# Eight column orders for the moving operands of the up- and down-projection matmuls

## The chip, the cores and the metric

The kernel runs on one core of a Trainium2 chip. The metric is the device time of one launch in microseconds. Three timed runs of the kernel before gave 1766.06, 1766.77 and 1769.52 us (median 1766.77 us). The profile is of one further execution.

## What is computed

Batch 8, sequence 3136, model width 256, feed-forward width 1024; x is float32, and the feed-forward weights are double precision. A spectral layer comes first, then a gated feed-forward layer with a convolution of three taps along the sequence:

```python
X = np.fft.rfft(x, axis=1)
Yr = Xr @ w_r - Xi @ w_i + b_r
Yi = Xr @ w_i + Xi @ w_r + b_i
Y  = soft_threshold(Yr, 0.01) + 1j * soft_threshold(Yi, 0.01)
x  = np.fft.irfft(Y, n=3136, axis=1)

h = np.maximum(x @ w_in, 0)                     # up-projection, 256 -> 1024
conv_out = sum(conv_w[k] * hp[:, k:k+S] for k in range(3))   # hp: h with a zero at each end
gate = 1 / (1 + np.exp(-conv_out))
out  = (h * gate) @ w_out                       # down-projection, 1024 -> 256
```

## The kernel before

The program has two parts. The first (to about 550 us) does the transforms and the channel mix as matmuls: L245 and L260 (stage 1), L280 (stage 2), L304 (mix) and L331 (stage 3), with results sent through device memory. The second part, where the change lies, runs the last transform (L423, plain float32) and the feed-forward layer.

In the second part the sequence lies along the free axis. `y` holds the transformed input of one batch item twice, `yh` (rounded to the type float32r, a 4-byte number that TensorE takes in one pass) and `yl` (what the rounding left), each with 128 channels on the partitions, two tiles of channels, and 3168 columns. The weights `win` and `wout` are likewise held as a rounded part and a rest.

The work is cut into 28 chunks of two pieces of 448 positions, and each chunk into 8 blocks `f` of 128 feed-forward channels: 224 steps. A step does the following.

- `up(f, ...)`: for each of the two pieces, six matmuls at L442 into one PSUM bank of the tile `ps_h` (two tiles of channels, times the three products high x high, high x rest, rest x high). The weights of the block are the stationary operand; 450 columns of `yh` or `yl` (448 and one neighbour at each end) are the moving operand, read in order and written to 450 PSUM columns in order. So twelve matmuls of 450 columns for a step.
- ScalarE and VectorE make the activation from it: ReLU out of PSUM into `h` (L444), the three taps (L447 or L449, L451), the sigmoid (L452), the product (L453), and its split into `gh` and `gl` (L456, L457).
- `down(ci, f, ...)`, four steps behind `up` (`LAG = 4`): for each of seven groups of 128 positions, three matmuls at L470. The activation is stationary; 256 columns of `wout`, block f, are moving, and the 256 results are added to half a bank of the accumulators `acc`, in which all eight blocks f are summed. So twenty-one matmuls of 256 columns for a step. After the last block, ScalarE copies the accumulators out (L479) and a DMA stores them.

The order on each engine is made by a scheduler that works from a modelled timeline. TensorE's stream alternates between the twelve matmuls of an `up` and the twenty-one of a `down`, with groups of sixteen L423 matmuls between them for the next batch item. The two PSUM banks of `ps_h` exist twice, so that the next `up` fills one pair while L444 reads the other.

Of the kernel before, what the change touches and what calls it, by code (L numbers as in the profile page):

```python
# [31 lines left out]
CH = 448  # L32
# [64 lines left out]
def spectral_ffn_kernel(ctx: ExitStack, tc: tile.TileContext, x, w_r, w_i, b_r, b_i,  # L97
                        w_in, conv_w, w_out, fwd1, fwd2, inv1, inv2, out):
    nc = tc.nc
# [316 lines left out]
    def stage4(b, jg, y):  # L416
# [10 lines left out]
        def view(q):  # L427
            return q[:, :, 1:S + 1].rearrange("p t (m j) -> p t m j", j=H)[:, :, :, jg * JG:(jg + 1) * JG]
        nc.scalar.copy(view(y[0]), src)
        nc.vector.tensor_tensor(view(y[1]), src, view(y[0].bitcast(F32)), op=ALU.subtract)  # L430

    def up(f, halves):
        ps = psh.tile([P, 2, 512], F32, name="ps_h", tag="ps_h")
        w = slice(f * P, (f + 1) * P)
        for a, (y, c0) in enumerate(halves):
            mm = []
            for t in range(NT):
                mm.append((win[0][:, t, w], y[0][:, t, c0:c0 + CH + 2]))
                mm.append((win[0][:, t, w], y[1][:, t, c0:c0 + CH + 2]))
                mm.append((win[1][:, t, w], y[0][:, t, c0:c0 + CH + 2]))  # L440
            for n, (lt, rh) in enumerate(mm):
                nc.tensor.matmul(ps[:, a, 0:CH + 2], lt, rh, start=(n == 0), stop=(n == len(mm) - 1))  # L442
        h = hp.tile([P, 2, CH + 2], F32, name="h")
        nc.scalar.activation(h, ps[:, :, 0:CH + 2], AF.Relu)  # L444
        c = wk.tile([P, 2, CH], F32, name="c", bufs=3)
        if f in TAP_DVE:
            nc.vector.tensor_scalar_mul(c, h[:, :, 0:CH], cw[:, 0, f:f + 1])  # L447
        else:
            nc.scalar.mul(c, h[:, :, 0:CH], cw[:, 0, f:f + 1])  # L449
        for k in (1, 2):  # L450
            nc.vector.scalar_tensor_tensor(c, h[:, :, k:k + CH], cw[:, k, f:f + 1], c, op0=ALU.mult, op1=ALU.add)  # L451
        nc.scalar.activation(c, c, AF.Sigmoid)  # L452
        nc.vector.tensor_tensor(c, h[:, :, 1:CH + 1], c, op=ALU.mult)  # L453
        gh = wk.tile([P, 2, CH], F32R, name="gh", bufs=5)
        gl = wk.tile([P, 2, CH], F32R, name="gl", bufs=5)
        nc.scalar.copy(gh, c)  # L456
        nc.vector.tensor_tensor(gl, c, gh.bitcast(F32), op=ALU.subtract)  # L457
        return [q.rearrange("p a n -> p (a n)") for q in (gh, gl)]
# [4 lines left out]
    def down(ci, f, gs, acc):  # L463
        gh, gl = gs
        if f == 0:
            acc = [pso.tile([P, 2, D], F32, name=f"acc{k}") for k in range((NM + 1) // 2)]
        for m in range(NM):
            sl = slice(m * P, (m + 1) * P)
            for n, (lt, rh) in enumerate(((gh, wout[0]), (gh, wout[1]), (gl, wout[0]))):
                nc.tensor.matmul(acc[m // 2][:, m % 2, :], lt[:, sl], rh[:, f, :], start=(f == 0 and n == 0 and m % 2 == 0),  # L470
                                 stop=(f == NF - 1 and n == 2), skip_group_check=True)
        if f == NF - 1:
            o = io.tile([P, NM, D], F32, name="o", bufs=1)
            for k, q in enumerate(acc):
                w = min(2, NM - 2 * k)
                if ci == NCH - 1 and k % 2:
                    nc.vector.tensor_copy(o[:, 2 * k:2 * k + w, :], q[:, 0:w, :])
                else:
                    nc.scalar.copy(o[:, 2 * k:2 * k + w, :], q[:, 0:w, :])  # L479
                if ci == NCH - 1:  # L480
                    nc.sync.dma_start(outv[:, ci * NM + 2 * k:ci * NM + 2 * k + w, :], o[:, 2 * k:2 * k + w, :])
            if ci < NCH - 1:
                nc.sync.dma_start(outv[:, ci * NM:(ci + 1) * NM, :], o)
        return acc
# [16 lines left out]
    for st in range(n_st + LAG):  # L501
        if st < n_st:
            ci, f = divmod(st, NF)
            hv = [divmod(2 * ci + a, NH) for a in range(2)]
            if f == 0:
                nb = hv[1][0] + 1
                if nb < B and nb not in ys and hv[0][0] == hv[1][0]:
                    ys[nb] = new_y(nb)
                    todo = [(nb, jg) for jg in range(NPC)]
            gs[st] = up(f, [(ys[b], a * CH) for b, a in hv])  # L510
            if todo and f in (1, 4, 7):
                b, jg = todo.pop(0)
                stage4(b, jg, ys[b])
        if st >= LAG:
            ci, f = divmod(st - LAG, NF)
            accs = down(ci, f, gs.pop(st - LAG), accs)
# [24 lines left out]
```

## Time and profile before

| | before |
|---|---|
| median of three timed runs | 1766.77 us |
| the profiled execution as timed | 1769.05 us |
| its span in the trace | 1767.3 us |
| mean granted TensorE clock | 0.995 |
| first L442 matmul | 574.0 us |
| last L470 matmul starts | 1762.7 us |

Each group of the profile's table stands for one line, one engine and one pair of operands: `out<-in`, the partitions and columns, the count, then the busy time in us and the mean duration of one in ns, then the idle time in front of it. Successive matmuls overlap, so a mean duration is longer than the time from one start to the next; the chain of work that ended last has its pieces cut so that they follow one another.

### The profile page before, as it was taken

The numbers are of one execution on the slowest core, as the hardware profiler recorded it, in microseconds if no ns is written. First come the engines' busy times: TensorE is split into PE (matmuls) and PEld (weight loads), VectorE is DVE, ScalarE is ACT, GpSimd is POOL, SyncE is SP. The second block draws the span as 40 slices with busy tenths as digits, with TensorE's granted clock in tenths as the row PEclk, the third lists the DMA queues.
The fourth block names the chain that finished last, engine by engine and source line by source line (L and its number), as shares of the span: only waits on it lengthen the run. The fifth ranks groups of instructions, "written<-read, shape, count | busy, mean of one in ns | idle before, by whom it ended". The sixth has DMA issues, their size and how long they took to land.

```text
span 1767.3 us, 29387 instructions
## 1 busy us (share of the span) xinstructions
PE 1731.0 (98%) x12096; PEld 1621.6 (92%) x12096; DVE 1524.3 (86%) x1820; ACT 1229.1 (70%) x1590; POOL 134.7 (8%) x60
## 2 busy tenths in 40 slices
PE   6899999999998999999999999999999999999999
PEld 2788888888998999999999999999999999999998
DVE  2899999998896988988888888888888888888887
ACT  2667777776665777777777777777777777777766
POOL 0122222222232000000000000000000000000000
PEclk8999999999999999999999999999999999999999
DMA  9777677677534110111111011111101111100001
GB/s 263 216 230 236 196 232 216 192 230 228 164 111 136 43 43 22 32 53 53 32 53 53 22 55 51 49 46 52 43 22 43 53 43 43 42 22 22 22 22 42
DMA packets 107382, 164.63 MB, mean 93 GB/s; under 512 B 8816, under 2 KB 86000, under 8 KB 107248
## 3 DMA queue, kind: packets, MB, share of 16 engines
q1 hardware_dynamic: 107248, 162.74, 30.9%
q8 instruction: 96, 1.57, 0.4%
q14 instruction: 38, 0.31, 0.1%
HBM read 85.65 MB, written 77.07 MB: 92 GB/s over the span
## 4 chain that ended last, share of the span: by engine, by line
PE 93%; DMA 3%; DVE 1%; ACT 1%; issue 0%; SPq 0%; ACTq 0%
PE acc L470 31%; PE ps_h L442 31%; PE ps_mx L304 12%; PE ps_s L423 5%; PE ps_s L280 5%; PE ps_s L331 4%; PE ps_s L245 4%; DMA i_raw<-in_inv_dram 2%; DMA z<-sc 1%; DMA sc<-ha 0%; DMA a<-sc 0%; DMA sc<-a 0%; ACT a L246 0%; DVE cw L212 0%; DVE yl L430 0%
## 5 line engine op out<-in xcount | busy, mean ns | idle before, releaser
L470 PE MATMUL acc<-wout,gh 128*128 128x256 f32 x3136 | 567.0, 280 | 0.0
L451 DVE SCALAR_TENSOR_TENSOR c<-h,cw,c 128x896 f32<-128x896 f32 x448 | 513.1, 1147 | 47.3 <-ACT c L449 46.3
L442 PE MATMUL ps_h<-yh,win 128*128 128x450 f32 x1792 | 551.0, 368 | 0.1
L470 PEld LDWEIGHTS acc<-wout,gh 128*128 128x128 f32 x3136 | 493.7, 188 | 6.5
L470 PE MATMUL acc<-wout,gl 128*128 128x256 f32 x1568 | 437.6, 281 | 0.0
L444 ACT ACTIVATE h<-ps_h 128x900 f32<-128x900 f32 x224 | 207.7, 927 | 254.8 <-PE ps_h L442 254.8
L442 PEld LDWEIGHTS ps_h<-yh,win 128*128 128x128 f32 x1792 | 338.7, 189 | 26.4 <-DVE yl L430 0.8
L442 PE MATMUL ps_h<-yl,win 128*128 128x450 f32 x896 | 329.2, 367 | 0.0
L470 PEld LDWEIGHTS acc<-wout,gl 128*128 128x128 f32 x1568 | 293.7, 188 | 0.1
L457 DVE TENSOR_TENSOR gl<-c,gh 128x896 fp32r<-128x896 f32 x224 | 243.1, 1089 | 53.6 <-ACT gh L456 50.1
L453 DVE TENSOR_TENSOR c<-h,c 128x896 f32<-128x896 f32 x224 | 243.6, 1088 | 46.9 <-ACT c L452 46.7
L456 ACT CAST gh<-c 128x896 fp32r<-128x896 f32 x224 | 209.8, 942 | 49.4 <-DVE c L453 49.4
L452 ACT ACTIVATE c<-c 128x896 f32<-128x896 f32 x224 | 213.3, 952 | 23.9 <-DVE c L451 21.0
L304 PE MATMUL ps_mx<-wmix_lo,fh 128*128 128x256 f32 x672 | 202.2, 301 | 0.0
L304 PE MATMUL ps_mx<-wmix_hi,fh 128*128 128x256 f32 x672 | 196.9, 294 | 0.5 <-DVE v L313 0.3
L304 PE MATMUL ps_mx<-wmix_hi,fl 128*128 128x256 f32 x672 | 188.7, 282 | 1.3 <-DVE fl L288 1.2
L442 PEld LDWEIGHTS ps_h<-yl,win 128*128 128x128 f32 x896 | 168.9, 189 | 11.0
L449 ACT ACTIVATE c<-h,cw 128x896 f32<-128x896 f32 x168 | 175.5, 1044 | 2.6 <-DVE gl L457 0.2
L321 POOL TENSOR_TENSOR sl<-v,sh 128x1024 fp32r<-128x1024 f32 x56 | 134.5, 2402 | 423.1 <-PE ps_s L331 300.0
L313 DVE TENSOR_TENSOR v<-ps_mx,p 64x512 f32<-64x512 f32 x224 | 154.0, 688 | 3.3
L304 PEld LDWEIGHTS ps_mx<-wmix_lo,fh 128*128 128x128 f32 x672 | 126.4, 188 | 12.3 <-issue 12.3
L304 PEld LDWEIGHTS ps_mx<-wmix_hi,fl 128*128 128x128 f32 x672 | 126.0, 188 | 11.8 <-issue 9.9
(84 smaller groups left out, 2023.0 us busy)
## 6 DMA issues: line engine op xcount, KB each, us to landing
a<-sc SPq DMA_DIRECT2D x56, 448.0 KB, 5.0
sc<-z SPq DMA_DIRECT2D x56, 448.0 KB, 3.3
z<-sc SPq DMA_DIRECT2D x56, 448.0 KB, 3.8
xr<-in_x_dram SPq DMA_DIRECT2D x55, 448.0 KB, 4.7
out_dram<-o SPq DMA_DIRECT2D x27, 896.0 KB, 4.0
sc<-a SPq DMA_DIRECT2D x49, 448.0 KB, 4.9
sc<-ha SPq DMA_DIRECT2D x7, 448.0 KB, 7.5
win_bits<-in_moe_w_in_dram SPq DMA_DIRECT2D x4, 512.0 KB, 7.6
```

Source lines behind the costliest of these rows:

```text
L304: nc.tensor.matmul(ps[c][:, k, :], lt, rh, start=(n == 0), stop=(n == len(mm) - 1))
L313: nc.vector.tensor_tensor(v[dst, :, k, :], ps[c][src], p1[src, c], op=ALU.add)
L321: SL_ENG.tensor_tensor(sl, v, sh.bitcast(F32), op=ALU.subtract)
L442: nc.tensor.matmul(ps[:, a, 0:CH + 2], lt, rh, start=(n == 0), stop=(n == len(mm) - 1))
L444: nc.scalar.activation(h, ps[:, :, 0:CH + 2], AF.Relu)
L449: nc.scalar.mul(c, h[:, :, 0:CH], cw[:, 0, f:f + 1])
L451: nc.vector.scalar_tensor_tensor(c, h[:, :, k:k + CH], cw[:, k, f:f + 1], c, op0=ALU.mult, op1=ALU.add)
L452: nc.scalar.activation(c, c, AF.Sigmoid)
L453: nc.vector.tensor_tensor(c, h[:, :, 1:CH + 1], c, op=ALU.mult)
L456: nc.scalar.copy(gh, c)
L457: nc.vector.tensor_tensor(gl, c, gh.bitcast(F32), op=ALU.subtract)
L470: nc.tensor.matmul(acc[m // 2][:, m % 2, :], lt[:, sl], rh[:, f, :], start=(f == 0 and n == 0 and m % 2 == 0), stop=(f == NF - 1 and n == ...
```

## The change

Two tables, `UP_WALK` and `DOWN_WALK`, give for each block f a pair (b, n), and `walk` views a run of columns as (a, b, n) and then goes over b first, a second, n last. The same view is put on the moving operand and on the PSUM output of a matmul, so each result goes to the column where it went before, and the columns are only visited in another order: n neighbours, a jump over b x n columns, and so on to the end, then again from the next group of n. Block 0 keeps the plain order.

| f | up: run of n columns, jump | down: run of n columns, jump |
|---|---|---|
| 0 | plain | plain |
| 1 | 2, 18 columns (72 bytes) | 2, 4 columns (16 bytes) |
| 2 | 2, 30 (120) | 2, 8 (32) |
| 3 | 2, 50 (200) | 2, 16 (64) |
| 4 | 2, 150 (600) | 2, 32 (128) |
| 5 | 10, 50 (200) | 2, 128 (512) |
| 6 | 30, 150 (600) | 16, 32 (128) |
| 7 | 50, 150 (600) | 64, 128 (512) |

```diff
+    UP_WALK = (None, (9, 2), (15, 2), (25, 2), (75, 2), (5, 10), (5, 30), (3, 50))
+    DOWN_WALK = (None, (2, 2), (4, 2), (8, 2), (16, 2), (64, 2), (2, 16), (2, 64))
+
+    def walk(ap, run):
+
+        return ap if run is None else ap.rearrange("p (a b n) -> p b a n", b=run[0], n=run[1])
+
     def up(f, halves):
...
             for n, (lt, rh) in enumerate(mm):
-                nc.tensor.matmul(ps[:, a, 0:CH + 2], lt, rh, start=(n == 0), stop=(n == len(mm) - 1))
+                nc.tensor.matmul(walk(ps[:, a, 0:CH + 2], UP_WALK[f]), lt, walk(rh, UP_WALK[f]), start=(n == 0), stop=(n == len(mm) - 1))
...
             for n, (lt, rh) in enumerate(((gh, wout[0]), (gh, wout[1]), (gl, wout[0]))):
-                nc.tensor.matmul(acc[m // 2][:, m % 2, :], lt[:, sl], rh[:, f, :], start=(f == 0 and n == 0 and m % 2 == 0),
+                nc.tensor.matmul(walk(acc[m // 2][:, m % 2, :], DOWN_WALK[f]), lt[:, sl], walk(rh[:, f, :], DOWN_WALK[f]), start=(f == 0 and n == 0 and m % 2 == 0),
                                  stop=(f == NF - 1 and n == 2), skip_group_check=True)
```

The new lines move L442 to L449 and L470 to L477. The next rows show TensorE's program at one place of the second part, where the `down` of block 7 is interrupted by the `up` of block 3; `win_78` and `win_79` are the rounded part and the rest of `win`, `wout_80` and `wout_81` those of `wout`. Before:

```order
L470 MATMUL acc_7735<-wout_80,gh 128x256
L470 MATMUL acc_7735<-wout_81,gh 128x256
L470 MATMUL acc_7735<-wout_80,gl 128x256
L442 MATMUL ps_h<-yh,win_78 128x450
L442 MATMUL ps_h<-yl,win_78 128x450
L442 MATMUL ps_h<-yh,win_79 128x450
```

The same place with the change:

```order
L477 MATMUL acc_7735<-wout_80,gh 128x2x2x64
L477 MATMUL acc_7735<-wout_81,gh 128x2x2x64
L477 MATMUL acc_7735<-wout_80,gl 128x2x2x64
L449 MATMUL ps_h<-yh,win_78 128x25x9x2
L449 MATMUL ps_h<-yl,win_78 128x25x9x2
L449 MATMUL ps_h<-yh,win_79 128x25x9x2
```

No row has moved; the shape of the operand has become 25 x 9 x 2 and 2 x 2 x 64 (b, a, n) in place of 450 and 256. Some steps on, again on TensorE, the `down` of block 2 ends and the `up` of block 7 begins:

```order
L477 MATMUL acc_8148<-wout_80,gh 128x4x32x2
L477 MATMUL acc_8148<-wout_81,gh 128x4x32x2
L477 MATMUL acc_8148<-wout_80,gl 128x4x32x2
L449 MATMUL ps_h<-yh,win_78 128x3x3x50
L449 MATMUL ps_h<-yl,win_78 128x3x3x50
L449 MATMUL ps_h<-yh,win_79 128x3x3x50
```

These stood there before as rows of 256 and 450 columns of L470 and L442. On the other engines the rows are the same, in the same order, but for the line numbers.

## The prediction

> **What bounds the kernel now.** I read the page's busy shares and its chain of waits first, since they say which engine sets the end and on which lines.
>
> ```profile
> span 1767.3 us, 29387 instructions
> PE 1731.0 (98%) x12096; PEld 1621.6 (92%) x12096; DVE 1524.3 (86%) x1820; ACT 1229.1 (70%) x1590; POOL 134.7 (8%) x60
> ...
> PE 93%; DMA 3%; DVE 1%; ACT 1%; issue 0%; SPq 0%; ACTq 0%
> PE acc L470 31%; PE ps_h L442 31%; PE ps_mx L304 12%; PE ps_s L423 5%; PE ps_s L280 5%; PE ps_s L331 4%; PE ps_s L245 4%; DMA i_raw<-in_inv_dram 2%; DMA z<-sc 1%; DMA sc<-ha 0%; DMA a<-sc 0%; DMA sc<-a 0%; ACT a L246 0%; DVE cw L212 0%; DVE yl L430 0%
> ```
>
> TensorE is the chain: 93% of the span, and two lines, the up-projection L442 and the down-projection L470, hold 31% each. These are the two lines that the change rewrites, so whatever it does to a matmul's pace is multiplied by thousands. Next I asked for the busy time of the whole feed-forward part, from the first L442 matmul at 574.0 us to the end, and for who waits there.
>
> ```profile
> core 0: us, PE busy (x) PEld busy (x) DVE busy (x) ACT busy (x) POOL busy (x), PEclk, DMA share, GB/s
> 574.00:1767.30 1193.30, 1188.88 (x8147) 1143.87 (x8146) 1034.19 (x1026) 855.76 (x998) 0.00 (x0) 1.00 0.13 40
> ```
>
> ```profile
> ACT h L444 <- PE ps_h L442: 254.8, 175, 3.0
> ...
> PEld ps_h L442 <- DVE yl L430: 0.8, 2, 0.5
> ```
>
> TensorE is busy 1188.88 of 1193.30 us at full granted clock: 4.4 us idle, so there is no slack in which a slower matmul could hide. ScalarE spends 254.8 us waiting for L442's result, while the only wait on TensorE's side is 0.8 us of its weight loads; VectorE works 1034 of 1193 us. A slower TensorE therefore makes the others wait longer and the kernel longer, one for one; a faster one would have about 159 us before VectorE's own work (1034.19 us) becomes the bound.
>
> **What one matmul costs.** The page's mean durations must not be used for this: they are those of single, overlapping instructions. The chain of waits in a short stretch gives the pace.
>
> ```profile
> 1002.82 2.47 PE ps_h L442 x12
> 1005.29 2.48 PE acc L470 x21
> 1007.77 2.47 PE ps_h L442 x12
> 1010.24 2.48 PE acc L470 x21
> ```
>
> Columns are start, length and line in us: twelve up matmuls take 2.47 us (0.206 us each, against 0.368 in the table), twenty-one down matmuls 2.48 us (0.118 each, against 0.280). A step is one feed-forward block of one chunk; there are 28 chunks of 8 blocks, 224 steps, and 224 x 2.47 = 553 us and 224 x 2.48 = 556 us agree with 31% of 1767.3. The counts and sizes are in the table of groups:
>
> ```profile
> L470 PE MATMUL acc<-wout,gh 128*128 128x256 f32 x3136 | 567.0, 280 | 0.0
> ...
> L442 PE MATMUL ps_h<-yh,win 128*128 128x450 f32 x1792 | 551.0, 368 | 0.1
> ...
> L470 PE MATMUL acc<-wout,gl 128*128 128x256 f32 x1568 | 437.6, 281 | 0.0
> ...
> L442 PE MATMUL ps_h<-yl,win 128*128 128x450 f32 x896 | 329.2, 367 | 0.0
> ```
>
> Per column that is 2470/(12 x 450) = 0.457 ns up and 2480/(21 x 256) = 0.461 ns down: proportional to the columns, with next to nothing fixed per instruction. Now the same figure for matmuls that the change does not touch:
>
> ```profile
> 402.22 3.04 PE ps_mx L304 x26
> 405.26 1.42 PE ps_s L331 x12
> 406.68 0.86 PE ps_s L245 x2
> ```
>
> L304 and L331 also move 256 columns of the same rounded 4-byte type: 3040/(26 x 256) = 0.457 ns and 1420/(12 x 256) = 0.462 ns, with other operands, other PSUM tiles and other neighbours. L245 moves 512 columns of plain float32: 860/(2 x 512) = 0.840 ns, the slow pace of this trace for streams of such a length. So two paces exist, and what decides between them is the number type, not where the data lie or what the other engines do.
>
> **The change, part by part.**
>
> *Instructions, order, waits.* Each matmul stays one matmul of the same column count, with the same weights, and the programs of all engines hold the same rows in the same order; only line numbers and the shape of 7 in 8 of the L442 and L470 operands differ. No DMA, wait, weight load, ScalarE or VectorE instruction is added, removed or moved. Cost 0.
>
> *Block 0.* Its order is None for both projections: 28 x (2.47 + 2.48) = 139 us of matmuls as before. Cost 0.
>
> *Blocks with long runs.* Up has runs of 10, 30 and 50 columns (f = 5, 6, 7), down runs of 16 and 64 (f = 6, 7). A break comes at most every 10 columns; if each cost a whole column time, this would be (45 + 15 + 9) runs x 336 matmuls x 0.457 ns + (16 + 4) x 588 x 0.461 ns = 10.6 + 5.4 = 16 us. I take 0, for the reason below.
>
> *Blocks of pairs.* Up f = 1 to 4 and down f = 1 to 5 go in runs of two columns, 8 bytes, with jumps of 72 to 600 bytes (up) and 16 to 512 bytes (down). They hold 4 x 28 x 2.47 = 276.6 us and 5 x 28 x 2.48 = 347.2 us: 623.8 us of matmuls ride on the one thing that this trace does not show, the pace of a TensorE stream that is not contiguous. Every moving operand and every matmul output of the kernel before is contiguous. So I bound it from both sides.
>
> Lower end: the pace is set by the type, as the four lines above show, so a different order gains at most the spread between them: 0.461 against 0.457 ns, 1% of the 7 x 28 x 2.48 = 486 us of reordered down matmuls, 5 us. Upper end: the pairs go at the slow pace of the trace, L245's 0.840 ns. An up step then takes 12 x 450 x 0.840 = 4.54 us (+2.07), a down step 21 x 256 x 0.840 = 4.52 us (+2.04): 4 x 28 x 2.07 + 5 x 28 x 2.04 = 232 + 286 = +518 us.
>
> Between them stand the only scattered accesses of the trace, made by other engines: L429 and L430 read PSUM with 448 bytes between neighbours, where L444 reads it, and L457 reads SBUF, in a straight line.
>
> ```profile
> L457 DVE TENSOR_TENSOR gl<-c,gh 128x896 fp32r<-128x896 f32 x224 | 243.1, 1089 | 53.6 <-ACT gh L456 50.1
> ...
> L444 ACT ACTIVATE h<-ps_h 128x900 f32<-128x900 f32 x224 | 207.7, 927 | 254.8 <-PE ps_h L442 254.8
> ...
> L429 ACT CAST yh<-ps_s 128x896 fp32r<-128x896 f32 x56 | 64.6, 1156 | 10.1 <-PE ps_s L423 10.0
> L430 DVE TENSOR_TENSOR yl<-ps_s,yh 128x896 fp32r<-128x896 f32 x56 | 64.3, 1150 | 14.5 <-ACT yh L429 14.3
> ```
>
> VectorE loses 1150/1089 = 6%, ScalarE 1156/896 against 927/900 per element = 25%, although every single element there is a jump (and the other side of both instructions, the tile y, goes in runs of four). Carried over to 623.8 us that is +35 to +156 us. TensorE would jump at every second column, every 0.91 ns, while these two take 1.28 and 1.29 ns per element: so they do not prove its pace, but they are far nearer to no loss than to L245's 84%. I take **no cost** as the likeliest: the scattered rows lose little with a jump at every element, and pairs halve the jumps. Both ends stay in the range.
>
> [...]
>
> **The sum.** 0 + 0 + 0 + 0 against the profiled execution: 1769.05 us as timed, 1767.3 us of it span. The median of the three timed runs is 1766.77 us, with 1766.06 to 1769.52 around it, so the profile is no special run and the forecast is the median, **1767 us**.
>
> **The rivals.**
>
> 1. *Pairs starve the array* (slower). The place is the nine pair blocks; the price is the slow pace, +518 us, 2285 us. It decides as soon as one 8-byte visit takes longer than two column times, 0.91 ns. For it: TensorE's fast pace leaves no reserve that the trace shows. Against it: the scattered rows lose 6 to 25%, not 84%. Only in down-projection, whose jumps are all powers of two where up's are odd multiples of 8 bytes, it would be +286 us, 2053 us.
> 2. *A partial loss*, of the size that the scattered rows show, or one lost beat at some breaks: +35 to +156 us, 1802 to 1923 us; I name 1862 us. The extreme of one lost column time at every break is (4 x 225 + 69) x 336 x 0.457 ns + (5 x 128 + 20) x 588 x 0.461 ns = 149 + 179 = +328 us, 2095 us.
> 3. *Every broken order is slow*, long runs too: 7 x 28 x (2.07 + 2.04) = +806 us, 2573 us. Against it: with runs of 50 or 64 a jump comes once in 23 or 29 ns. [...]
> 4. *Faster*: at most the 5 us above, 1762 us. Nothing shortens a stream whose column count stays.
> 5. *The change does not do what it says*: not possible for the shapes, which are in the built program; but if the reordered pattern were walked as a contiguous one by the hardware, the time would be that of the forecast.
>
> **How the numbers follow.** No cost: 0.53. Partial loss, anything above 0.2% up to 2095 us: 0.19. Pairs slow in down alone: 0.07; in both: 0.12. Every order slow: 0.06. Faster: 0.03. About 0.2% (3.5 us) is what a measurement of this kernel can tell from no change; a loss of 0.6 ns per reordered matmul (3.5 us over 6468) is enough to leave that band. Hence faster 0.03, same 0.53, slower 0.44. The range runs from 1761 us (the gain bound) to 2100 us (one column time per break, and pairs slow in down alone); above it lie 0.18.
>
> **What would show it.** The new profile splits itself by shape: the chain's pieces give twelve up matmuls and twenty-one down matmuls for each block, and block 0 is the control. Right: all pieces stay at 2.45 to 2.50 us, ScalarE's wait for L444 stays near 255 us and TensorE's busy time near 1731 us. Rival 1 shows pieces of about 4.5 us for pair blocks alone and a wait of ScalarE that grows by hundreds of us; in down alone, only the twenty-ones grow. Rival 2 shows pieces of 2.6 to 3.1 us, growing with the number of runs if each break has a price. Rival 3 shows the runs of 50 and 64 slow as well. The forecast is wrong if any block's piece leaves 2.5 us by more than 0.02 us: 28 x 7 x 2 such pieces would be 8 us.

## The result

The changed kernel takes 2335.36 us (median of four runs, 2333.89 to 2336.66) against 1768.14 us: a ratio of 1.3193, 95% interval 1.3173 to 1.3212. The forecast was no change. The profiled execution has a span of 2334.3 us, 567 us more than before.

The page of the changed kernel, busy shares and chain:

```profile
span 2334.3 us, 29387 instructions
PE 2295.9 (98%) x12096; PEld 1891.9 (81%) x12096; DVE 1530.8 (66%) x1820; ACT 1232.2 (53%) x1590; POOL 134.7 (6%) x60
...
PE 95%; DMA 3%; DVE 1%; ACT 1%; issue 0%; SPq 0%; ACTq 0%; DVEq 0%
```

The same 12096 matmul records keep TensorE busy for 2295.9 us in place of 1731.0; VectorE and ScalarE do the same work in nearly the same time (1530.8 us after 1524.3, and 1232.2 after 1229.1) and only wait longer. The busy time from the first up matmul (576.6 us) to the end, and ScalarE's wait for the up-projection (L442 and L444 are now L449 and L451):

```profile
576.60:2334.30 1757.70, 1753.43 (x8146) 1413.09 (x8145) 1040.64 (x1026) 858.96 (x998) 0.00 (x0) 1.00 0.09 27
```

```profile
ACT h L451 <- PE ps_h L449: 817.5, 224, 8.1
...
PEld ps_h L449 <- issue: 180.3, 844, 0.2
```

The stage has grown from 1193.3 to 1757.7 us at full granted clock, so 564 of the 567 us lie in it, and ScalarE's wait has grown by 563 us. The 180.3 us of TensorE's weight loads stand under issue, which names no engine that they waited for. The chain of one chunk shows which blocks grew; columns are start, length and line, and the sixteen L423 records of the next batch item and the pieces of up block 5 and down blocks 0 and 1 are left out:

```profile
1383.71 2.47 PE ps_h L449 x12
1386.19 4.80 PE acc L477 x21
1390.99 5.09 PE ps_h L449 x12
...
1397.86 3.62 PE acc L477 x21
1401.48 5.12 PE ps_h L449 x12
1406.60 2.52 PE acc L477 x21
1409.13 5.08 PE ps_h L449 x12
1414.21 2.45 PE acc L477 x21
1416.66 3.54 PE ps_h L449 x12
...
1430.39 2.65 PE ps_h L449 x12
1433.05 4.90 PE acc L477 x21
1437.95 2.55 PE ps_h L449 x12
1440.50 4.61 PE acc L477 x21
```

The up pieces are blocks 0 to 4, then 6 and 7; the down pieces run four blocks behind: 4 to 7, then 2 and 3. Plain block 0 stays at 2.47 us for its twelve matmuls; pairs take 5.1 us, runs of 30 and 50 columns 2.65 and 2.55. Two blocks of pairs are much cheaper than the rest: up block 4 (3.54 us) and down block 5 (3.62 us).

The matmul starts in the trace, grouped by block, give the mean time from one start to the next in ns (each block has 336 up and 588 down matmuls). The two rows of visits are a count that is explained below:

| block f | 0 | 1 | 2 | 3 | 4 | 5 | 6 | 7 |
|---|---|---|---|---|---|---|---|---|
| up before | 206 | 206 | 207 | 206 | 206 | 206 | 205 | 205 |
| up after | 208 | 423 | 425 | 422 | 295 | 243 | 224 | 214 |
| up: visits to 16-byte lines x 1.83 ns | 207 | 411 | 411 | 411 | 411 | 247 | 219 | 214 |
| down before | 119 | 117 | 118 | 119 | 117 | 120 | 118 | 118 |
| down after | 120 | 231 | 232 | 220 | 230 | 173 | 121 | 118 |
| down: visits x 1.83 ns | 117 | 234 | 234 | 234 | 234 | 234 | 117 | 117 |

Added up against means of 205.8 and 118.2 ns: up pairs 741 ns x 336 = 249 us, up long runs 63 x 336 = 21 us, down pairs 494 x 588 = 291 us, down long runs 3 x 588 = 2 us; together 562 of the 567 us.

### The profile page after: what moved, and what is told of

Its sections match the earlier page's. It is cut to its first block, busy times and chain, and to the rows that moved or that the text cites. A ratio compares the mean times of both kernels' runs of the same rounds, so it can differ in the third digit from the quotient of the medians.

```text
span 2334.3 us, 29387 instructions
## 1 busy us (share of the span) xinstructions
PE 2295.9 (98%) x12096; PEld 1891.9 (81%) x12096; DVE 1530.8 (66%) x1820; ACT 1232.2 (53%) x1590; POOL 134.7 (6%) x60
## 4 chain that ended last, share of the span: by engine, by line
PE 95%; DMA 3%; DVE 1%; ACT 1%; issue 0%; SPq 0%; ACTq 0%; DVEq 0%
PE acc L477 36%; PE ps_h L449 35%; PE ps_mx L304 9%; PE ps_s L423 4%; PE ps_s L280 4%; PE ps_s L245 3%; PE ps_s L331 3%; DMA i_raw<-in_inv_dram 1%; DMA wm_raw<-in_w_i_dram 0%; DVE v L313 0%; DMA z<-sc 0%; DMA xr<-in_x_dram 0%; DMA sc<-ha 0%; DMA a<-sc 0%; PE ps_s1h L260 0%
## 5 line engine op out<-in xcount | busy, mean ns | idle before, releaser
L477 PE MATMUL acc<-wout,gh 128*128 128x256 f32 x3136 | 815.5, 353 | 0.0
L449 PE MATMUL ps_h<-yh,win 128*128 128x450 f32 x1792 | 743.1, 479 | 0.0
L451 ACT ACTIVATE h<-ps_h 128x900 f32<-128x900 f32 x224 | 206.7, 923 | 817.5 <-PE ps_h L449 817.5
L477 PEld LDWEIGHTS acc<-wout,gh 128*128 128x128 f32 x3136 | 581.3, 198 | 67.3 <-issue 26.3
L477 PE MATMUL acc<-wout,gl 128*128 128x256 f32 x1568 | 551.3, 353 | 0.0
L449 PEld LDWEIGHTS ps_h<-yh,win 128*128 128x128 f32 x1792 | 356.1, 199 | 170.9 <-issue 126.1
L449 PE MATMUL ps_h<-yl,win 128*128 128x450 f32 x896 | 428.5, 478 | 0.0
L477 PEld LDWEIGHTS acc<-wout,gl 128*128 128x128 f32 x1568 | 310.2, 198 | 17.3 <-issue 0.2
L449 PEld LDWEIGHTS ps_h<-yl,win 128*128 128x128 f32 x896 | 178.1, 199 | 74.7 <-issue 54.2
L304 PE MATMUL ps_mx<-wmix_lo,fh 128*128 128x256 f32 x672 | 202.2, 301 | 0.0
L304 PE MATMUL ps_mx<-wmix_hi,fh 128*128 128x256 f32 x672 | 196.9, 294 | 0.5 <-DVE v L313 0.3
L304 PE MATMUL ps_mx<-wmix_hi,fl 128*128 128x256 f32 x672 | 188.6, 282 | 1.3 <-DVE fl L288 1.2
L304 PEld LDWEIGHTS ps_mx<-wmix_lo,fh 128*128 128x128 f32 x672 | 126.4, 188 | 12.3 <-issue 12.3
L304 PEld LDWEIGHTS ps_mx<-wmix_hi,fl 128*128 128x128 f32 x672 | 126.1, 188 | 11.8 <-issue 9.9
```

Source lines behind the costliest of these rows:

```text
L304: nc.tensor.matmul(ps[c][:, k, :], lt, rh, start=(n == 0), stop=(n == len(mm) - 1))
L449: nc.tensor.matmul(walk(ps[:, a, 0:CH + 2], UP_WALK[f]), lt, walk(rh, UP_WALK[f]), start=(n == 0), stop=(n == len(mm) - 1))
L477: nc.tensor.matmul(walk(acc[m // 2][:, m % 2, :], DOWN_WALK[f]), lt[:, sl], walk(rh[:, f, :], DOWN_WALK[f]), start=(f == 0 and n == 0 and ...
```

## The experiments

The **line theory** came out of that table. It supposes that TensorE fetches the moving operand in lines of 16 bytes, four float32r columns, and that a visit to a line takes as long as four columns of the plain stream, 4 x 0.457 = 1.83 ns, however few of its columns are used. The size and the price are an estimate of mine, fitted to the table: pairs take twice the plain time (423 against 206 ns up), runs of 10, 30 and 50 columns 18, 9 and 4% more. Straight on, 450 columns are 113 visits and 256 are 64. In pairs they are 225 and 128. A run of 10 starting 0 or 8 bytes into a line covers 3 lines, 135 visits in all; runs of 30 and 50 cover 8 and 13 lines, 120 and 117 visits; aligned runs of 16 and 64 need no extra visit. But for up block 4 and down block 5 the counts lie within about 6% of the measured pace. Rivals: the loss is in the PSUM writes; or each jump has a price (some 0.9 ns), wherever it lands.

**Reads or writes.** In the first kernel only the moving operand is walked, in the second only the output; the other side is `plain`, the same three-dimensional view without the exchange of a and b. The line theory prices reads alone: by it the first kernel keeps the whole loss and the second has none of it.

```diff
-  nc.tensor.matmul(walk(ps[:, a, 0:CH + 2], UP_WALK[f]), lt, walk(rh, UP_WALK[f]), ...
+  nc.tensor.matmul(plain(ps[:, a, 0:CH + 2], UP_WALK[f]), lt, walk(rh, UP_WALK[f]), ...     # reads only
+  nc.tensor.matmul(walk(ps[:, a, 0:CH + 2], UP_WALK[f]), lt, plain(rh, UP_WALK[f]), ...     # writes only
```

> Only the moving operand is walked in the eight orders; the PSUM output is written straight on, so the sums land in permuted columns (computation changed there). Line theory (TensorE fetches the moving operand in 16-byte lines at 1.83 ns a visit, as long as four columns of 0.457 ns, however few columns a visit uses): the whole loss stays, about 2335 us, pair blocks 0.42 us per up and 0.23 us per down matmul. PSUM theory (the loss is in the 8-byte writes): about 1767 us, all up matmuls 0.206 us. Shared: something between.

> Only the PSUM output is walked; the moving operand is read straight on, so the sums land in permuted columns (computation changed there). [...] PSUM theory: about 2335 us. If any broken write pattern slows a matmul, down blocks 1 to 5 stand at 0.2 us and more.

Reads only: 2334.16 us, ratio 1.3182 (1.3146 to 1.3218). Writes only: 1769.84 us, ratio 0.9998 (0.9985 to 1.0011). The chain of the reads-only kernel, and then of the writes-only kernel:

```profile
1130.69 4.79 PE acc L481 x21
1135.49 5.06 PE ps_h L453 x12
```

```profile
1107.79 2.47 PE ps_h L453 x12
1110.26 2.47 PE acc L481 x21
1112.73 2.47 PE ps_h L453 x12
```

With the reads walked, each block has the pace of the changed kernel within 0.3 ns; with the writes walked, each has the pace of before. The whole loss is on the read side, and none of these orders costs anything in PSUM (ratio 0.9998).

**Whole lines, and the same runs moved by 8 bytes.** Up is plain; down goes in runs of four (f = 1 to 5) and eight columns (f = 6, 7). The second kernel lays `wout` 8 bytes further, so that every run straddles a line border.

```diff
+    UP_WALK = (None, None, None, None, None, None, None, None)
+    DOWN_WALK = (None, (2, 4), (4, 4), (8, 4), (16, 4), (32, 4), (4, 8), (8, 8))
...
-    wout = [cst.tile([P, NF, D], F32R, name=f"wout_{q}") for q in range(2)]
+    wout = [cst.tile([P, NF, D + 4], F32R, name=f"wout_{q}")[:, :, 2:D + 2] for q in range(2)]    # second kernel
```

> Up plain; down in runs of four columns with jumps of 32, 64, 128, 256 and 512 bytes (f = 1 to 5) and of eight columns with jumps of 128 and 256 bytes (f = 6, 7), read and written alike; each run of four is one whole 16-byte line. Line theory: every down matmul keeps 0.117 us, total about 1767 us. Jump theory (each break costs about 0.9 ns, as the pair blocks of 225 and 128 runs would give): runs of four 117 + 64 x 0.9 = 175 ns, f = 6 and 7 146 ns, total + (5 x 58 + 2 x 29) ns x 588 = +205 us, 1970 us.

> As the runs of four and eight before, but the down weights lie 8 bytes later, so each run straddles line borders; the same number of jumps. Line theory: a run of four touches two lines, 128 visits, 0.234 us for f = 1 to 5; a run of eight touches three, 96 visits, 0.175 us for f = 6, 7; plain block 65 visits, 0.119 us; total + (5 x 117 + 2 x 58) ns x 588 = +412 us, about 2180 us, unless the line visited last but a few is kept. Jump theory: the same as without the shift.

Aligned: 1791.77 us, ratio 1.0120 (1.0103 to 1.0137). Moved by 8 bytes: 2144.55 us, ratio 1.2111 (1.2078 to 1.2144). By block, in ns:

| block f | 0 | 1 | 2 | 3 | 4 | 5 | 6 | 7 |
|---|---|---|---|---|---|---|---|---|
| run, jump in bytes | plain | 4, 32 | 4, 64 | 4, 128 | 4, 256 | 4, 512 | 8, 128 | 8, 256 |
| aligned | 119 | 118 | 115 | 127 | 135 | 130 | 117 | 121 |
| moved by 8 bytes | 121 | 232 | 226 | 224 | 246 | 173 | 177 | 181 |

The chain of the aligned kernel shows down blocks 1 and 2 and, further on, block 4:

```profile
1118.74 2.47 PE acc L477 x21
1121.22 2.47 PE ps_h L449 x12
1123.69 2.42 PE acc L477 x21
...
1135.49 2.83 PE acc L477 x21
```

The chain of the kernel with the moved weights shows blocks 4, 5 and 6 with plain up pieces between them:

```profile
1120.96 5.26 PE acc L479 x21
1126.22 2.46 PE ps_h L451 x12
1128.68 3.57 PE acc L479 x21
1132.25 2.46 PE ps_h L451 x12
1134.71 3.74 PE acc L479 x21
```

The jumps are as many and as long in both kernels; 8 bytes of position make up 353 us. So it is the visits to lines that are paid, not the jumps: two visits for a run of four (224 to 246 ns in blocks 1 to 4, expected 234), three for a run of eight (177 and 181, expected 176). Two findings were not expected. Aligned lines are not all alike: jumps of 128 to 512 bytes cost 8 to 14%, all of the 21 us by which the aligned kernel is slower, while jumps of 64 bytes are 2% faster than the straight order (115 against 118 ns). And block 5 of the second kernel, which comes back to a line after only one other run, pays less than its visits (173 ns against 234).

**How long a line is kept.** All blocks in pairs, with the number of pairs in a cycle varied.

```diff
+    UP_WALK = (None, (75, 2), (45, 2), (25, 2), (15, 2), (9, 2), (5, 2), (3, 2))
+    DOWN_WALK = (None, (64, 2), (32, 2), (16, 2), (8, 2), (4, 2), (2, 2), (2, 4))
```

> All reordered blocks in pairs; the number of other lines visited between the two visits to one line is varied: up f = 1 to 7 comes back to a line after 3, 5, 9, 15, 25, 45, 75 pairs, down f = 1 to 6 after 2, 4, 8, 16, 32, 64 pairs; down f = 7 is runs of four with a jump of 32 bytes. Line theory without any memory of lines: 225 visits x 1.83 = 0.41 us up and 128 x 1.83 = 0.234 us down everywhere. With a few lines kept, as the two short cycles of the changed kernel suggest (0.294 us after 3, 0.173 after 2): the pace rises from there to the full price between 4 and 9 pairs and stays; up after 5 between 0.30 and 0.42, down after 4 between 0.173 and 0.22. If instead the length of the jump decides, the jumps of 360 bytes (up, 5) and 256 bytes (down, 4) cost as the others do. Total near 2400 us.

It took 2578 us in a single run; the expected 2400 us was badly added up (the paces that were expected give about 2550 us). The paces by block came as follows. Up, cycles of 3, 5, 9, 15, 25, 45 and 75 pairs: 297, 429, 423, 424, 419, 399 and 398 ns. Down, cycles of 2, 4, 8, 16, 32 and 64: 168, 227, 229, 217, 235 and 229 ns, and 120 for runs of four. (In both lists the program's first reordered block comes first.) The chain has the up cycles of 3 and of 5 pairs on either side of a down piece:

```profile
1283.06 3.59 PE ps_h L449 x12
1286.65 4.89 PE acc L477 x21
1291.55 5.12 PE ps_h L449 x12
```

It looks as if a line were kept across one or two other visits, and then only part of the time: 297 ns are 162 visits' worth where 225 are made and 113 lines exist. From four or five pairs on next to nothing is left of it (227 ns down, 429 up). In this run the shortest cycles also have the longest jumps (600 and 512 bytes). That the return to the line counts, and not the long jump, is argued from whole lines, where jumps of 512 bytes took 130 ns and not less than the plain 118.

**Plain float32.** Up and down plain; the stage-1 and stage-2 matmuls, whose pace is 0.844 ns per column, are walked in singles, pairs and fours.

```diff
+    run = (None, (16, 1), (16, 2), (16, 4))[(2 * jc + j // 2) % 4]           # stage 1, 512 columns
+    run = (None, (4, 1), (4, 2), (4, 4))[k]                                  # stage 2, 128 columns
```

> Up and down plain; the plain-float32 matmuls of the first part are walked, read and written alike: of each four neighbours one plain, one in single columns, one in pairs, one in runs of four (stage 1, 512 columns, jumps of 16 columns per n; stage 2, 128 columns, jumps of 4 n). Their pace is 0.844 ns per column, so four columns take 3.37 ns and a pair 1.69 ns. Line theory (a visit 1.83 ns, hidden where the array needs longer): stage 1 plain 432 ns, singles 512 x 1.83 = 937, pairs 468, fours 432; stage 2 plain 112, singles 234, pairs 117, fours 112; total about +55 us, 1822 us. Jump theory (0.9 ns per break added): stage 1 singles 893, pairs 662, fours 547 ns. If the loss was a factor of two on whatever is broken: pairs 864.

> As the float32 kernel, but only the PSUM output is walked, so the transforms' results land in permuted columns (computation changed there). If PSUM takes any order at these paces, single columns too: stage 1 432 and stage 2 112 ns everywhere, 1767 us. [...]

Both sides walked: 1813.1 us, a single run. Each float32 matmul stands in the trace as two records (196 of L245 before, for 98 results that ScalarE copies out), each float32r matmul as one (2688 of L442, for 224 steps of twelve). From the start of the first to that of the second (medians in ns): stage 1 plain 433, singles 842, pairs 439, fours 432; stage 2 plain 111, singles 212, pairs 135, fours 108. The chain shows a plain matmul of stage 1 and one in singles, each with its two records (L250 is L245 of before):

```profile
207.54 0.86 PE ps_s L250 x2
...
212.44 1.72 PE ps_s L250 x2
```

Only the output walked: 1769.29 us in a single run, against 1769.57 us for the kernel before, 432 and 112 ns everywhere. So single columns of float32 cost a visit each, about 1.65 ns by these starts (842/512 and 212/128), less than the 1.83 ns I had put; pairs in stage 1 are nearly free (439 against 433 ns), since by the line theory a visit is covered by the 1.69 ns that two columns take there anyway, and a factor of two (864 ns) or a price per jump (662 ns) is out. In stage 2 pairs stand 24 ns above plain, where 5 were expected, but only in the first record, which follows on a matmul in singles. From the pairs' second record to the next matmul it is 117 ns, as the line theory has it, and from the singles' second record to the pairs 228 ns, 1.78 ns a column. So the pairs agree, and a part of the price of the singles seems to fall into the gap behind them; no run tests that. PSUM took even single columns in any order at this pace (432 and 112 ns, where the singles that were also read in that order took 842 and 212). Two columns to a visit are nearly enough for float32 in this trace (439 against 433 ns in stage 1, 117 against 111 in stage 2 for the second record); for float32r they give half the pace (423 against 206 ns), and even the 3.3 that runs of ten make on average cost 18% (243 ns).

**The order that was faster.** Jumps of 64 bytes in runs of four for all down blocks; then the same in the mix (L304) and stage 3 (L331) too; then on the output alone.

```diff
+    UP_WALK = (None, None, None, None, None, None, None, None)
+    DOWN_WALK = ((4, 4), (4, 4), (4, 4), (4, 4), (4, 4), (4, 4), (4, 4), (4, 4))
...
+    nc.tensor.matmul(walk(ps[c][:, k, :], (4, 4)), lt, walk(rh, (4, 4)), ...             # second kernel, mix
+    nc.tensor.matmul(walk(ps[:, k, :], (4, 4)), lt[:, u, :], walk(rh[:, k, :], (4, 4)), ...   # stage 3
```

> Up plain; every down block in runs of four columns with a jump of 64 bytes, the one order that stood below the plain pace in the runs of four (115 against 118 ns mean). If that is real, 4704 x 3 ns = 14 us less, about 1755 us (0.8% faster); if it was only the neighbours of that block, no change within 0.2%.

> As the down blocks in runs of four with a jump of 64 bytes, and the same order also for the mix (2016 matmuls) and the third transform stage (672 matmuls), which move 256 columns of float32r too. If that order reads 2 to 3 ns faster wherever 256 such columns are moved: 2688 x 2.1 ns = 6 us less again, about 1751 us; if it helped only in the down projection, 1757 us.

> Only the PSUM output of the down projection goes in runs of four with a jump of 64 bytes; the read is straight on, so the sums land in permuted columns (computation changed there). If the gain of that order comes from the read, 117 ns and about 1769 us, no change; if from the write, 114 ns and about 1757 us.

Down alone: 1756.74 us, ratio 0.9933 (0.9919 to 0.9947), with its twenty-one matmuls in 2.42 us in place of 2.48:

```profile
1014.61 2.42 PE acc L477 x21
1017.03 2.46 PE ps_h L449 x12
1019.49 2.42 PE acc L477 x21
```

This kernel computes the same result and is faster than the kernel before. 224 x 0.06 = 13 us agrees with the measured 13 us. On the output alone: 1770.76 us, ratio 0.9999 (0.9990 to 1.0007), so the gain too comes from the read. With the mix and stage 3 as well: 1765.87 us, ratio 0.9984 (0.9961 to 1.0008): their pace falls (mix 117 to 115 ns in the median), but the first part ends later, the first up matmul starting at 579.4 us against 572.5 us (572.5 to 577.9 us in the traces of kernels with an unchanged first part). One VectorE line of the first part, in the kernel with down alone and then in this one:

```profile
L288 DVE TENSOR_TENSOR fl<-d,fh 128x512 fp32r<-128x512 f32 x56 | 40.7, 726 | 0.7 <-ACT fh L287 0.4
...
L292 DVE TENSOR_TENSOR fl<-d,fh 128x512 fp32r<-128x512 f32 x56 | 50.6, 904 | 0.7 <-ACT fh L291 0.4
```

In this kernel's trace 13 of the 56 take 0.8 to 2.8 us in place of 0.69 us; each of them overlaps a GpSimd instruction (L325) and ends 0.55 us after it. With down alone there are 3 such. From 400 to 440 us half of the chain is VectorE's, where it was TensorE's alone. So a faster mix seems to have moved two other engines into each other's way; no run tests this.

**Which jumps are good.** Down moves whole aligned lines from a wider stretch of `wout`, sixteen lines in a cycle unless said, with the jump varied; PSUM is written straight on.

```diff
+    def lines(q, run):
+        if run is None:
+            return q[:, 0, :]
+        jump, a = run
+        flat = q.rearrange("p f d -> p (f d)")[:, 0:4 * jump * a]
+        return flat.rearrange("p (a j n) -> p j a n", a=a, n=4)[:, 0:64 // a]
+    DOWN_WALK = (None, (4, 16), (8, 16), (16, 16), (32, 16), (8, 8), (16, 4), (5, 16))      # first
+    DOWN_WALK = (None, (6, 16), (7, 16), (9, 16), (10, 16), (12, 16), (20, 16), (24, 16))   # second
```

> Up plain; down moves whole 16-byte lines in an order where the jump and the number of lines between neighbours vary apart, PSUM written straight on, moving columns taken from other places of the weights (computation changed there). Sixteen lines in a cycle with jumps of 64, 128, 256 and 512 bytes (f = 1 to 4) and 80 bytes (f = 7), eight lines with 128 (f = 5), four lines with 256 (f = 6); the last two stood at 127 and 134 ns with both sides walked. If the length of the jump decides: f = 1 and 7 115, f = 2 127, f = 3 134, f = 4 130 ns or more. If the short cycle decides (coming back to the neighbourhood of a line after 4 or 8 visits): f = 1 to 4 and 7 all 115 to 118, f = 5 127, f = 6 134 ns.

> As the run on jumps of whole lines, sixteen lines in a cycle, with jumps of 96, 112, 144, 160, 192, 320 and 384 bytes (f = 1 to 7; moving columns taken from other places of the weights, PSUM written straight on: computation changed there). Known so far in this order: 64 bytes 115, 80 bytes 136, 128 bytes 124, 256 and 512 bytes 143 ns. If the pace grows with the jump alone: 125 to 145, in order. If jumps that are a multiple of 64 bytes are the good ones: 192, 320 and 384 at 115 to 125, the others near 136. If no rule: scattered, and the second order stays open.

A single run each, 1830.67 and 1797.77 us. Mean ns by jump in bytes: 64: 115; 80: 137; 96: 153; 112: 117; 128: 124; 144: 116; 160: 126; 192: 119; 256: 144; 320: 115; 384: 125; 512: 143. Cycles of eight lines with 128 bytes gave 127, of four with 256 bytes 134. So the jump decides more than the cycle (at 256 bytes the cycle of sixteen took 144 ns), but neither its length alone nor a multiple of 64 is the rule, which stays open.

## Why the prediction was wrong

- *What bounds the kernel* held: TensorE had no slack, the loss went one for one into the end (564 us in the stage, 567 in the span), and VectorE and ScalarE only waited (ScalarE for the up-projection 817.5 us, after 254.8).
- *Instructions, order, waits* and *block 0* held: the same counts, plain pieces of 2.47 us.
- *Blocks of pairs* is the step that failed: "I take **no cost** as the likeliest". The runs showed 249 us up and 291 us down. The argument carried scattered reads of PSUM by ScalarE and VectorE, one number every 1.28 ns, over to SBUF reads by TensorE, which, counted in lines, uses one up every 1.83 ns with four columns of it and would have needed one every 0.91 ns with two. I saw that gap and weighed it too lightly. "What decides between them is the number type, not where the data lie" was drawn from contiguous streams alone: there 0.457 ns per column and 1.83 ns per line are the same pace, and the trace of before could not tell them apart.
- *Blocks with long runs* were put at 0, with 16 us as the extreme; measured 23 us. Runs of 10 columns, which end inside a line, took 243 ns, near the 247 of their visits; a price of one column time per break, 206 + 45 x 0.457 = 227 ns, was the wrong form.
- *Rival 1*, pairs at the slow pace, was right in place and sign and near in size (2285 us, 12%). Its price was borrowed from L245 (0.84 ns per column), where it goes with plain float32 read straight on; pairs took 0.94 up and 0.90 down, so that its total came near is partly luck. Up block 4 and down block 5 came cheaper (295 and 173 ns), as if a line were still partly held after one or two other pairs, and long runs added their 23 us.
- *Rival 1 in down alone* fails: up and down pay alike, odd or even jumps. *Rival 3* fails as a rule on any broken order: the price follows the lines visited, from nothing (runs of 64, 118 ns as before) to double (pairs, 423 against 206 ns). *Rivals 2, 4 and 5* fail for this change. That no order could gain ("at most the 5 us") fails for another one: runs of four at 64 bytes gain 13 us.
- *The range* ended at 2100 us, since rival 1 in both projections had 0.12 and was left outside.

## What to carry to other kernels

In these runs the time of a matmul went by the 16-byte lines that its moving operand visited, about 1.83 ns for each with float32r. The stream kept its pace within 3% where every visit used all four columns of an aligned line and the jump was 32 or 64 bytes (118 and 115 ns against 118), and in pairs it halved (423 against 206 ns up, 231 against 118 down). Even whole lines took up to 30% longer with some jumps (153 ns at 96 bytes). The order in which the results go to PSUM cost nothing in any run that walked the output alone (ratios 0.9998 and 0.9999, and 1769.29 against 1769.57 us with float32 down to single columns), so if columns have to be permuted, do it in the output and keep the read straight. Evidence on access patterns from one engine and memory should not be carried to another: ScalarE and VectorE lost 25% and 6% on scattered PSUM reads, most of TensorE's pairs about 100%. The straight streams would have said how much reserve there is: they use a line up every 1.83 ns with float32r, and pairs cost double; every 3.38 ns (433/128) with float32 in stage 1, and pairs cost 1%.

## What the hardware showed that I had not expected

- The straight order is not the fastest: lines visited with jumps of 64 bytes took 115 against 118 ns for 256 columns, other jumps between 115 and 153 ns.
- A line just visited seems to be partly kept: with one other pair between two visits 168 to 173 ns where the count of visits gives 234, with two 295 to 297 where it gives 411; from cycles of four pairs down (217 to 235 ns) and five up (398 to 429) nothing certain.
- A visit is not one fixed time: 1.65 to 1.78 ns for single float32 columns, 1.70 to 1.90 ns for pairs of float32r, 1.80 for lines at 64 bytes.
